# Attention visits of TensorE that carry two pairs, and a product kept in SBUF, in a fused attention and two-layer kernel

## Chip, cores and metric

The kernel runs on one NeuronCore of a Trainium2 chip. The metric is device time in microseconds (us). The engines are named as in the profile: PE is TensorE (matrix products), DVE is VectorE, ACT is ScalarE, POOL is GpSimd, SP is SyncE, which here only issues DMAs.

## What is computed

Three layers follow one another. The first is a linear attention with a decayed state, for 4 batches, 8 heads, 768 steps and a head width of 48:

```
state = alpha[t, :, None] * state + outer(k[t], v[t])      # 48 x 48 per batch and head
y[t]  = q[t] @ state
```

The 8 heads side by side give 3072 tokens of 384 numbers. The second layer is `h = x @ w_in` (384 to 2048), `g = h * cos(h)`, `g @ w_out` (back to 384). The third is `h = max(x @ w1, x @ w2, x @ w3)` (384 to 768), then `h @ w_out`. All data are float32.

## The kernel before, in words

The tokens are cut into six units of 512 (`u` = 0 to 5). A unit of attention is made of four pairs of heads (`p`), so there are 24 pairs; unit 0 has a form of its own (`att0`), and 20 pairs run through `att`. Each has a chunked form of the recurrence. Two scans on DVE (L501, L506) make the decay factors, POOL multiplies them into k and q (L505, L508), PE transposes k (L513) and ACT copies the result to SBUF as `kt` (L516). Then comes a first visit of PE, `akmm`, with 32 products of k and q (L525) and 32 of k and v (L529) in two banks of PSUM. DVE masks the scores into `a` (L534), POOL and DVE bring the state forward (L539 to L551), ACT lays copies of half the state beside it as `z` (L549). A second visit of PE, `values` (L559, L566: 64 small products), makes the outputs in two more banks, and ACT and DVE split them into a high and a low part, in the tile `xt` (L582, L584). Pair 3 of a unit goes through `yy` and is spread over the other three by small DMAs (L591).

The small products use a quarter of the PE array each. The large ones are 128 by 128 by 512 columns. Every factor of the layers is split in a high and a low part, so one product is three of these: high by high, high by low, low by high.

`moe1(i)` is one of the 96 steps of the second layer, 16 for each unit. Nine large products (L604 to L606, three chunks of the inner dimension) fill one PSUM bank with h. ACT makes a whole number from it (L612), DVE reduces the argument (L613), ACT takes the sine (L614), DVE multiplies it with h *into the same bank* (L620), ACT rounds the product to `gh` (L621) and DVE takes the rest as `gl` from the bank (L626). In the steps 0 to 3 the product is kept in the SBUF buffer `q` (L616) and POOL makes the rest. Nine more large products (L631 to L633) add to three accumulators. After the 16th step of a unit the accumulators are emptied through one buffer `yy` to DRAM (L640 to L643). The weights of the second layer come in 32 blocks (L344); ACT, DVE and POOL turn each into a high and a low part (L345 to L354) while the first steps already run. The third layer (`moe2_h`, `moe2_o`, L682 to L710) follows.

PSUM has eight banks. Three are the accumulators; the other five (`NBANK`) are handed out by a planner to h, to the transposes ("t"), to the two visits ("r", "y") and to others, with a limit for each kind (`LIMIT`).

The order of all the work is set before the kernel is built. `Program.op` records every operation with an engine, an estimated duration, what it reads and writes, and a due time in steps. `Program.order` plays these through with a model of the engines, the banks, the DMAs, PE's clock, and the reading of PE's instructions in blocks of 256, takes for each engine the ready operation with the smallest due time, and so fixes one order for each engine. On the chip an engine keeps that order and waits wherever an operand isn't there yet.

Of the kernel before, what the change touches and what calls it, by code (L numbers as in the profile page):

```python
# [26 lines left out]
P = 128  # L27
C = 64
# [24 lines left out]
NQ, NG, NRAW, NRAW1, NTOP, NIN, NKQ, NV, NGS = 3, 2, 3, 4, 2, 3, 2, 3, 3  # L53
# [6 lines left out]
RYS = 9  # L60


GLE1 = 0
# [3 lines left out]
XLE = 3  # L67
MKP = 0
GATE, GSTEP = 1, 2
LOD = (1, 3)  # L70

W1E = 6
MOE_EARLY = 3
EARLY = 1
FIRST = -4
ATT0 = -1
ATTS = 3.3

# [4 lines left out]
class Program:  # L83
# [38 lines left out]
    def order(self, banks, limit):  # L122
# [31 lines left out]
        never = float("inf")  # L154

# [3 lines left out]
        def ready(i):  # L159
            t = ready_at[i]  # L160
            need = opens.get(i, ())
            if need:

                t = max(t, sorted(freed_at[need[0][1]])[len(need) - 1], sorted(bank_free)[len(need) - 1])
            if self.ops[i][6]:
                t = max(t, port_free)
            return t

        for _ in range(n):
# [3 lines left out]
            i = min((self.ops[j][5], j) for j in waiting[e] if ready(j) <= t)[1]  # L173
            waiting[e].remove(i)
            _, dur, nbytes, _, _, _, port, tiled, count = self.ops[i]
            start[i] = t
            if e == "PE":
                if tiled != mode:
                    dur += SWITCH
                    mode = tiled  # L180
                if t - free[e] > IDLE:
                    cold = t + COLD
                dur += min(dur, max(0.0, cold - t) / 2)
                issued += count
                if issued >= block:
                    late = max(0.0, fetched - t - dur * (1.0 - (issued - block) / count))
                    dur += late
                    fetched = t + dur + (FETCH[1] if dma_free > t + dur else FETCH[0])
                    block += BLOCK
# [23 lines left out]
            for u in users[i]:  # L213
# [3 lines left out]
                if not left[u]:  # L217
                    waiting[self.ops[u][0]].append(u)
        self.start, self.end = start, ended
# [15 lines left out]
def mm(n, m):  # L235
    return (n + 0.375 * m) / 2400.0
# [16 lines left out]
def dma(nbytes):  # L253
    return max(nbytes, 15e3)
# [6 lines left out]
HW, LANDED, SLACK = 0.46, 1.6, 5.0  # L261
# [3 lines left out]
def tile_kernel(ctx, tc, aa, qk, vv, wt, outT):  # L265
# [36 lines left out]
    d_b = [ap.tile([PR, 2, N2, D], F32, name=f"d{i}") for i in range(2)]  # L302
    z_b = [ap.tile([PR, N2, D], F32, name=f"z{i}") for i in range(2)]
    kt_b = [ap.tile([P, N2, PR], F32, name=f"kt{i}") for i in range(2)]
# [70 lines left out]
    def att0(k, p, t0):  # L375
        na, nk, nv, n2 = k % NIN, k % NKQ, k % NV, k % 2
        t, kq_, v, kt, s = al_b[na], kq_b[nk], v_b[nv], kt_b[n2], s_b[p]
        vk, kk_ = ("v", nv), nk
        gf, kg = g_b[k % NGS], ("g", k % NGS)
        if k == 2:  # L380
            v, vk = q_b[2][:, 0:2 * N2 * D].rearrange("p (i j e) -> p i j e", i=N2, j=2), ("q", 2)
            kq_, kk_ = q_3.rearrange("p a b -> p (a b)")[0:PR, 0:2 * HB], "q01"
# [10 lines left out]
        tk, sk = ("kt", n2), ("s", p)  # L393
# [87 lines left out]
    def att(u, k, p, t0):  # L481
        m = u * NP + k
        n2, na, nk, nv = m % 2, m % NIN, m % NKQ, m % NV
        t, kq_, v, kt, a, s, d, z, iv = al_b[na], kq_b[nk], v_b[nv], kt_b[n2], a_b[n2], s_b[p], d_b[n2], z_b[n2], inv0[n2]
        vk, kk_ = ("v", nv), nk

        gf, kg = g_b[m % NGS], ("g", m % NGS)
        g = gf.rearrange("p (c t) -> p c t", c=NC)
        fv = t[:, 0:AL].rearrange("p (c t) -> p c t", c=NC)
        kv, qv = kq_[:, 0:HB], kq_[:, HB:]  # L490
        kv3, qv3 = (x.rearrange("p (c t) -> p c t", c=NC) for x in (kv, qv))
        kf, kk, kq = ("inf", na), ("ink", kk_), ("inq", kk_)
        ik, tk, dk = ("iv", n2), ("kt", n2), ("d", n2)
        sk = [("s", p, j) for j in range(2)]
        half = [slice(UP * h, UP * h + D) for h in range(2)]
        first = t0
        op("SP", HW, lambda: nc.sync.dma_start(t, aa[u, p, :, 0:KO]), (), [kf], first - 4.8 + (0.8 if not k else 0), dma(PR * KO * 4), tiled=True)
        op("SP", HW, lambda: nc.sync.dma_start(kq_, qk[u, p]), (), [kk, kq], first - 3.9, dma(PR * 2 * HB * 4), tiled=True)
        op("SP", HW, lambda: nc.sync.dma_start(v, vv[u, p]), (), [vk], first - 3.7, dma(P * HB * 3), tiled=True)
        gate = [("wil", GATE + GSTEP * k)] if u == 1 else []  # L500
        op("DVE", 0.07 + 0.00208 * AL, lambda: ve.tensor_tensor_scan(  # L501
            gf[:, ::-1], t[:, 1:AL + 1][:, ::-1], one0.rearrange("p c t -> p (c t)"), 0.0, ALU.mult, ALU.add), ["one0", kf, *gate], [(*kg, 0), (*kg, 1)], t0 - 1, port=True)
        kgs = [(*kg, 0), (*kg, 1)]
# [4 lines left out]
        op("Pool", pool(HB), lambda: ge.tensor_tensor(qv3, qv3, fv[:, :, 1:], ALU.mult), [kf], [kq], t0 - 1)  # L508
        pk_k, pk = psum("t")
# [5 lines left out]
        op("PE", N2 * 0.08, trans, [kk, "ident"], [pk_k], t0, count=2 * N2)  # L515
        op("Act", act(N2 * PR, True), lambda: se.activation(kt, pk[:, 0:N2 * PR].rearrange("p (a b) -> p a b", a=N2), AF.Copy), [pk_k], [tk], t0)  # L516
        rk, r = psum2("r")
        AO = N2 * D

        def akmm():  # L520
            for i in range(N2):
                for h in range(2):
                    for j in range(2):
                        c, w = 2 * i + h, slice(UP * j, UP * j + D)
                        pe.matmul(r[j][C * h:C * (h + 1), AO + i * C:AO + (i + 1) * C], kv3[w, c], qv3[w, c], start=True, stop=True)  # L525
            for i in range(N2):
                for h in range(2):
                    for j in range(2):
                        pe.matmul(r[h][half[j], i * D:(i + 1) * D], kt[C * h:C * (h + 1), i, UP * j:UP * j + D], v[C * h:C * (h + 1), i, j], start=True, stop=True)  # L529

        op("PE", N2 * (mm4(C) + mm4(D)), akmm, [kk, kq, tk, vk, ("done", n2)], rk, t0 + 0.2, tiled=True, count=128)
        for j in range(2):
            rv = r[j][:, AO:AO + N2 * C].rearrange("p (c t) -> p c t", c=N2)
            op("DVE", dve(HB // 2), lambda j=j, rv=rv: ve.tensor_tensor(a[:, j], rv, tri.to_broadcast([P, N2, C]), ALU.mult),  # L534
               [rk[j], "tri"], [("a", n2, j)], t0 + 0.2)

        kvs = [r[h][0:PR, 0:AO].rearrange("p (b e) -> p b e", b=N2) for h in range(2)]
        gs = [g.rearrange("p (b h) t -> p b h t", h=2)[:, :, h, 0:1].to_broadcast([PR, N2, D]) for h in range(2)]
        op("Pool", pool(N2 * D), lambda: ge.tensor_tensor(d[:, 0], s, gs[0], ALU.mult), [*kgs, *sk], [(dk, 0)], t0 + 0.2)  # L539
        op("DVE", dve(N2 * D), lambda: ve.tensor_tensor(s, kvs[0], d[:, 0], ALU.add), [rk[0], (dk, 0)], sk, t0 + 0.25)  # L540
        op("DVE", dve(N2 * D), lambda: ve.tensor_tensor(d[:, 1], s, gs[1], ALU.mult), [*kgs, *sk], [(dk, 1)], t0 + 0.25, port=True)
        qh = qv.rearrange("p (b h t) -> p b h t", b=N2, h=2)
        for h in range(2):
            w, x = half[h], half[1 - h]
            if u == 1:
                op("Pool", pool(HB // 2), lambda h=h, w=w, x=x: ge.tensor_copy(kv3[w, 0:N2], qh[x, :, h]), [kq], [kk], t0 + 0.25)
            else:
                op("Act", act(HB // 2), lambda h=h, w=w, x=x: se.activation(kv3[w, 0:N2], qh[x, :, h], AF.Copy), [kq], [kk], t0 + 0.25)
            op("Act", act(N2 * D), lambda h=h, w=w, x=x: se.activation(z[w], d[x, h], AF.Copy), [(dk, h)], [("z", n2, h)], t0 + 0.25)  # L549
        if u + 1 < NU:  # L550
            op("DVE", dve(N2 * D), lambda: ve.tensor_tensor(s, kvs[1], d[:, 1], ALU.add), [rk[1], (dk, 1)], sk, t0 + 0.27)  # L551

        yks, y = psum2("r" if u <= RYS else "y")

        def values():
            for i in range(N2):
                for h in range(2):
                    for j in range(2):
                        pe.matmul(y[h][half[j], i * C:(i + 1) * C], v[C * h:C * (h + 1), i, j], a[C * h:C * (h + 1), j, i],  # L559
                                  start=(i == 0), stop=False, skip_group_check=True)  # L560
            for i in range(N2):
                for h in range(2):
                    for j in range(2):
                        w = half[h]
                        dd, qq = (d[w, h, i], qh[w, i, h]) if j == h else (z[w, i], kv3[w, i])
                        pe.matmul(y[h][half[j], i * C:(i + 1) * C], dd, qq, start=False, stop=False, skip_group_check=True)  # L566

        op("PE", N2 * 2 * mm4(C), values,
           [vk, ("a", n2, 0), ("a", n2, 1), *[(dk, h) for h in range(2)], *[("z", n2, h) for h in range(2)], kq, kk], [*yks, ("done", n2)], t0 + 0.3, tiled=True, count=128)
        xa = []  # L570
# [346 lines left out]
```

## Time and profile before

| | |
|---|---|
| median of 3 runs | 780.68 us (780.45 to 780.71) |
| the profiled execution | 780.58 us |
| its span, first to last instruction | 778.7 us |
| PE busy | 768.0 us, 99% of the span, 5863 products |
| DVE, ACT, POOL busy | 55%, 45%, 16% |
| granted clock of PE | 1.00 in every stretch of 20 us but the last (0.96) |

The span is what the trace covers; 1.9 us of the execution lie outside it. PE's busy time is that of overlapping products whose ends are modelled, so how densely PE works is to be read from the distance of starts, not from this share.

### The profile page before, as it was taken

The numbers are of one execution on the slowest core, as the hardware profiler recorded it, in microseconds if no ns is written. First come the engines' busy times: TensorE is split into PE (matmuls) and PEld (weight loads), VectorE is DVE, ScalarE is ACT, GpSimd is POOL, SyncE is SP. The second block draws the span as 40 slices with busy tenths as digits, with TensorE's granted clock in tenths as the row PEclk, the third lists the DMA queues.
The fourth block names the chain that finished last, engine by engine and source line by source line (L and its number), as shares of the span: only waits on it lengthen the run. The fifth ranks groups of instructions, "written<-read, shape, count | busy, mean of one in ns | idle before, by whom it ended". The sixth has DMA issues, their size and how long they took to land.

```text
span 778.7 us, 14199 instructions
## 1 busy us (share of the span) xinstructions
PE 768.0 (99%) x5863; PEld 627.5 (81%) x5863; DVE 425.1 (55%) x718; ACT 348.4 (45%) x671; POOL 127.3 (16%) x133
## 2 busy tenths in 40 slices
PE   8999999999999999999999999999999999999998
PEld 6688887888888888887888888888888888888886
DVE  8889997767675777575567554531221312213121
ACT  5788865546554555555478544421211112111121
POOL 5555432110211111111043200300000000000000
PEclk9999999999999999999999999999999999999999
DMA  9866743212322222121047402320020200200001
GB/s 285 268 191 202 229 122 112 66 54 63 108 65 53 82 89 67 41 90 59 8 142 254 140 0 79 145 81 28 14 95 23 84 27 15 95 13 15 15 26 41
DMA packets 26464, 69.84 MB, mean 90 GB/s; under 512 B 3392, under 2 KB 6464, under 8 KB 26400
## 3 DMA queue, kind: packets, MB, share of 16 engines
q1 hardware_dynamic: 26400, 68.93, 27.7%
q8 instruction: 46, 0.75, 0.4%
q14 instruction: 18, 0.15, 0.1%
HBM read 52.80 MB, written 14.16 MB: 86 GB/s over the span
## 4 chain that ended last, share of the span: by engine, by line
PE 94%; DMA 3%; ACT 1%; DVE 1%; issue 0%; POOL 0%; SPq 0%; ACTq 0%; POOLq 0%; DVEq 0%
PE ps L682 9%; PE ps L683 9%; PE ps L684 9%; PE acc L631 9%; PE ps L604 8%; PE acc L633 8%; PE acc L632 8%; PE ps L605 8%; PE ps L606 8%; PE ps L705 3%; PE ps L707 3%; PE ps L706 3%; PE ps L525 2%; PE ps L559 1%; DMA raw<-in_wt 1%; PE ps L566 1%
## 5 line engine op out<-in xcount | busy, mean ns | idle before, releaser
L631 PE MATMUL acc<-gh,woh 128*128 128x512 f32 x288 | 116.0, 403 | 1.0 <-DVE yy L641 1.0
L604 PE MATMUL ps<-xt,wih 128*128 128x512 f32 x288 | 114.7, 398 | 1.0 <-ACT xt L474 0.8
L605 PE MATMUL ps<-xt,wih 128*128 128x512 f32 x288 | 112.3, 390 | 0.8 <-DVE xt L479 0.8
L632 PE MATMUL acc<-gh,wol 128*128 128x512 f32 x288 | 112.4, 390 | 0.0
L633 PE MATMUL acc<-gl,woh 128*128 128x512 f32 x288 | 112.2, 390 | 0.0
L606 PE MATMUL ps<-xt,wil 128*128 128x512 f32 x288 | 112.1, 389 | 0.0
L613 DVE SCALAR_TENSOR_TENSOR q<-q,ps 128x512 f32<-128x512 int32 x96 | 65.6, 683 | 46.9 <-ACT q L612 46.8
L612 ACT ACTIVATE q<-ps 128x512 int32<-128x512 f32 x96 | 57.2, 596 | 61.6 <-PE ps L606 61.3
L620 DVE TENSOR_TENSOR ps<-q,ps 128x512 f32<-128x512 f32 x92 | 63.7, 692 | 35.8 <-ACT q L614 35.7
L626 DVE TENSOR_TENSOR gl<-ps,gh 128x512 fp32r<-128x512 f32 x92 | 62.9, 687 | 35.6 <-ACT gh L621 35.0
L692 DVE TENSOR_TENSOR ps<-t,ps 128x512 f32<-128x512 f32 x36 | 25.0, 696 | 103.9 <-PE ps L684 103.8
L614 ACT ACTIVATE q<-q 128x512 f32<-128x512 f32 x96 | 60.6, 631 | 39.7 <-DVE q L613 39.4
L621 ACT ACTIVATE gh<-ps 128x512 fp32r<-128x512 f32 x92 | 54.8, 597 | 47.4 <-DVE ps L620 44.0
L693 ACT ACTIVATE h<-ps 128x512 fp32r<-128x512 f32 x36 | 21.6, 600 | 109.7 <-DVE ps L692 109.7
L631 PEld LDWEIGHTS acc<-gh,woh 128*128 128x128 f32 x288 | 54.0, 188 | 13.5 <-DVE yy L641 1.6
L604 PEld LDWEIGHTS ps<-xt,wih 128*128 128x128 f32 x288 | 54.1, 188 | 13.0 <-ACT xt L474 1.2
L633 PEld LDWEIGHTS acc<-gl,woh 128*128 128x128 f32 x288 | 54.1, 188 | 12.0 <-DVE gl L626 0.4
L690 DVE TENSOR_TENSOR t<-t,ps 128x512 f32<-128x512 f32 x36 | 24.8, 688 | 70.9 <-PE ps L684 70.2
L605 PEld LDWEIGHTS ps<-xt,wih 128*128 128x128 f32 x288 | 54.1, 188 | 11.4 <-DVE xt L479 1.1
L606 PEld LDWEIGHTS ps<-xt,wil 128*128 128x128 f32 x288 | 54.1, 188 | 11.4
L632 PEld LDWEIGHTS acc<-gh,wol 128*128 128x128 f32 x288 | 54.1, 188 | 9.9
L710 ACT ACTIVATE y<-ps 128x512 f32<-128x512 f32 x18 | 10.8, 600 | 93.2 <-PE ps L707 93.2
(148 smaller groups left out, 1427.8 us busy)
## 6 DMA issues: line engine op xcount, KB each, us to landing
raw<-in_wt SPq DMA_DIRECT2D x56, 384.0 KB, 3.5
kq<-in_qk SPq DMA_DIRECT2D x22, 448.0 KB, 4.5
x1d<-yy SPq DMA_DIRECT2D x18, 512.0 KB, 2.9
xt<-x1d SPq DMA_DIRECT2D x18, 512.0 KB, 4.2
al<-in_aa SPq DMA_DIRECT2D x23, 228.4 KB, 3.3
outT<-y SPq DMA_DIRECT2D x18, 256.0 KB, 2.0
v<-in_vv SPq DMA_DIRECT2D x23, 192.0 KB, 4.7
xt<-yy SPq DMA_DIRECT2D x30, 64.0 KB, 2.3
```

What stands on the lines that cost most here:

```text
L604: pe.matmul(ps, wi["h"][:, f, cc], xt[:, cc, 0], start=(cc == 0), stop=False)
L605: pe.matmul(ps, wi["h"][:, f, cc], xt[:, cc, 1], start=False, stop=False)
L606: pe.matmul(ps, wi["l"][:, f, cc], xt[:, cc, 0], start=False, stop=(cc == NR - 1))
L613: op("DVE", dve(HB), lambda: ve.scalar_tensor_tensor(q, q.bitcast(I32), -TWOPI, ps, ALU.mult, ALU.add), [hk], [qk], m)
L620: op("DVE", dve(HB), lambda: ve.tensor_tensor(ps, q, ps, ALU.mult), [qk], [hk], m)
L626: op("DVE", dve(HB), lambda: ve.tensor_tensor(gl, ps, gh.bitcast(F32), ALU.subtract), [hk, ("gh", gn)], [("gl", gn)], m)
L631: pe.matmul(acc[c], oh, gh, start=(f == 0), stop=False)
L632: pe.matmul(acc[c], ol, gh, start=False, stop=False)
L633: pe.matmul(acc[c], oh, gl, start=False, stop=(f == NF1 - 1))
L682: pe.matmul(ps, w2t["h"][m][:, f, cc], xt[:, cc, 0], start=(cc == 0), stop=False)
L683: pe.matmul(ps, w2t["h"][m][:, f, cc], xt[:, cc, 1], start=False, stop=False)
L684: pe.matmul(ps, w2t["l"][m][:, f, cc], xt[:, cc, 0], start=False, stop=(cc == NR - 1))
```

## The change

The diff does four things.

- The two visits of a pair are no longer two. From the second pair of unit 2 on, `visit(n, n - 1)` does the first products of pair n and, behind them in the same run of PE, the values of pair n - 1. It takes four of the five banks. The five visits of unit 1's pairs and of the first pair of unit 2 that hold first products alone stay separate, and so do the four values of unit 1 and the very last ones. The transposes and scans of a pair (`turn`) are due one step before its visit.
- From step 16 on (`GLQ`) DVE writes sine times h into the SBUF buffer `q`, and `gh` and `gl` are made from there.
- `d`, `z` and `kt` have one buffer in place of two, and `kq` three in place of two. In unit 0 the transposed k of every other pair lies in a buffer `q`, and one pair no longer borrows two of these.
- The planner's numbers change: a large product costs a little less, a visit has a fixed cost, DMAs of attention get no extra 5 us, a large visit that is overdue keeps others from opening a bank, a visit that would outrun the reading of instructions is put off. The weights of the second layer are due six steps earlier and their loads two steps more; two low parts of unit 0 are made by DVE and not by PE and ACT.

The diff, cut to its core:

```diff
-NQ, NG, NRAW, NRAW1, NTOP, NIN, NKQ, NV, NGS = 3, 2, 3, 4, 2, 3, 2, 3, 3
+NQ, NG, NRAW, NRAW1, NTOP, NIN, NKQ, NV, NGS, ND = 3, 2, 3, 4, 2, 3, 3, 3, 3, 1
-GLE1 = 0
+GLE1, GLQ = 0, 16
-XLE = 3
+XLE = 1
-GATE, GSTEP = 1, 2
+GATE, GSTEP = 1, 1
-W1E = 6
-MOE_EARLY = 3
-EARLY = 1
+W1E = 12
+MOE_EARLY = 4
+EARLY = 3
+VIS, VEND, VQ = 4.0, 13, 0.2
+LARGE, STALL, PATIENT = 2, 0.6, 1.5
+V2, V2S, TA = 16.0, 3.2, 1.0
+NA = (NU - 1) * NP
...
             if need:
-                t = max(t, sorted(freed_at[need[0][1]])[len(need) - 1], sorted(bank_free)[len(need) - 1])
+                for j, due in large.items():
+                    if due + PATIENT < self.ops[i][5] and ready_at[j] <= max(t, free[self.ops[i][0]]):
+                        return never
+                kinds = [k[1] for k in need]
+                t = max(t, sorted(bank_free)[len(need) - 1], *(sorted(freed_at[c])[kinds.count(c) - 1] for c in kinds))
...
-            i = min((self.ops[j][5], j) for j in waiting[e] if ready(j) <= t)[1]
+            def stall(j):
+                n, x = self.ops[j][8], block - issued
+                if n < 128 or x > n:
+                    return 0.0
+                return max(fetched - t - self.ops[j][1] * x / n, FETCH[0] - self.ops[j][1] * (1.0 - x / n) - 0.113 * max(0, BLOCK - n + x))
+
+            i = min((e == "PE" and stall(j) > STALL, self.ops[j][5], j) for j in waiting[e] if ready(j) <= t)[2]
...
 def mm(n, m):
-    return (n + 0.375 * m) / 2400.0
+    return (n + 0.25 * m) / 2400.0
...
-HW, LANDED, SLACK = 0.46, 1.6, 5.0
+HW, LANDED, SLACK = 0.46, 1.6, 0.0
...
+    def visit(an, yn, t0):
+        now, old = (x is not None for x in (an, yn))
...
+        rk, r = psum2("r") if now else ((), ())
+        yks, y2 = psum2("y") if old else ((), ())
...
+            reads += [("ink", nk), ("inq", nk), ("kt",), ("v", nv)]
+            dur, count = dur + 0.87, count + 128
...
+            reads += [("v", nvo), *[("a", yn % 2, j) for j in range(2)], *[(("d", yn % ND), h) for h in range(2)],
+                      *[("z", h) for h in range(2)], ("inq", nko), ("ink", nko)]
+            dur, count = dur + 0.96, count + 128
+
+        def all_parts():
+            if now:
+                akmm()
+            if old:
+                values()
+
+        op("PE", dur, all_parts, reads, sorted({*keys}), t0, tiled=True, count=count)
...
-        if GLE1 <= i < GLP1:
+        if i >= GLQ:
+            op("DVE", dve(HB), lambda: ve.tensor_tensor(q, q, ps, ALU.mult), [hk], [qk], m)
+            op("Act", act(HB), lambda: se.activation(gh, q, AF.Copy), [qk], [("gh", gn)], m)
+            op("DVE", dve(HB), lambda: ve.tensor_tensor(gl, q, gh.bitcast(F32), ALU.subtract), [qk, ("gh", gn)], [("gl", gn)], m, port=True)
+        elif GLE1 <= i < GLP1:
...
+        plan = []
+        for n in range(NP):
+            t = ATT0 + ATTS * n
+            plan += [(t, n, None, t), (t + 0.1, None, n, t + 0.1)]
+        plan += [(t, n, n - 1 if n > NP else None, t - TA) for n, t in ((n, V2 + V2S * (n - NP)) for n in range(NP, 2 * NP))]
+        plan += [(t, n if n < NA else None, n - 1, t - TA) for n, t in ((n, NF1 + VEND + VIS * (n - 2 * NP)) for n in range(2 * NP, NA + 1))]
+        for t, an, yn, tt in plan:
+            if an is not None:
+                at(max(tt - 0.01, FIRST + NP), turn, an, tt)
+            at(max(t, FIRST + NP), visit, an, yn, t)
```

The bodies of `akmm()` and `values()` are those of before, and the operations of DVE, ACT and POOL behind them too; in a visit of two pairs they stand in the order: masks of the new scores, outputs of the old pair, then the state of the new pair.

## Rows read from the trace of the kernel before

**Rows 1.** Page: busy time, share of the span, instructions by engine

```profile
PE 768.0 (99%) x5863; PEld 627.5 (81%) x5863; DVE 425.1 (55%) x718; ACT 348.4 (45%) x671; POOL 127.3 (16%) x133
```

**Rows 2.** Waits of PE: us in total, times, longest one

```profile
PE acc L631 <- DVE yy L641: 1.0, 1, 1.0
PE ps L525 <- ACT kt L516: 1.0, 1, 1.0
PE ps L605 <- DVE xt L479: 0.8, 1, 0.8
PE ps L604 <- ACT xt L474: 0.8, 1, 0.8
```

**Rows 3.** Timeline of PE: first large product, and one undisturbed run (start, duration)

```profile
24.75 0.40 PE L604 MATMUL ps<-xt,wih 128*128 128x512 f32 x1
...
161.09 0.39 PE L604 MATMUL ps<-xt,wih 128*128 128x512 f32 x1
...
163.58 0.39 PE L606 MATMUL ps<-xt,wil 128*128 128x512 f32 x1
```

**Rows 4.** Timeline of PE: a visit of first products between large products

```profile
152.27 0.39 PE L606 MATMUL ps<-xt,wil 128*128 128x512 f32 x1
152.59 0.69 PE L525 MATMUL ps<-kq 48*64 48x64 f32 x32
153.10 0.54 PE L529 MATMUL ps<-v,kt 64*48 64x48 f32 x32
153.57 0.50 PE L631 MATMUL acc<-gh,woh 128*128 128x512 f32 x1
...
154.37 0.40 PE L631 MATMUL acc<-gh,woh 128*128 128x512 f32 x1
```

**Rows 5.** Timeline of PE: the same pair's visit of values

```profile
156.88 0.39 PE L606 MATMUL ps<-xt,wil 128*128 128x512 f32 x1
157.19 0.67 PE L559 MATMUL ps<-a,v 64*48 64x64 f32 x32
...
158.09 0.22 PE L566 MATMUL ps<-kq,d 48*48 48x64 f32 x1
158.24 0.50 PE L604 MATMUL ps<-xt,wih 128*128 128x512 f32 x1
...
159.04 0.40 PE L631 MATMUL acc<-gh,woh 128*128 128x512 f32 x1
```

**Rows 6.** Timeline of ACT: a step of the second layer begins

```profile
163.33 0.60 ACT L612 ACTIVATE q<-ps 128x512 int32<-128x512 f32 x1 [0.67 <-PE ps L606]
```

**Rows 7.** Timeline of DVE: the same step

```profile
163.96 0.69 DVE L613 SCALAR_TENSOR_TENSOR q<-q,ps 128x512 f32<-128x512 int32 x1 [0.58 <-ACT q L612]
165.35 0.70 DVE L620 TENSOR_TENSOR ps<-q,ps 128x512 f32<-128x512 f32 x1 [0.70 <-ACT q L614]
166.71 0.69 DVE L626 TENSOR_TENSOR gl<-ps,gh 128x512 fp32r<-128x512 f32 x1 [0.66 <-ACT gh L621]
```

**Rows 8.** Groups of DVE by line and form: busy us, mean ns, idle before

```profile
L506 DVE TENSOR_TENSOR_SCAN al<-al,inv 112x520 f32<-112x520 f32 x20 | 25.4, 1271 | 0.9
```

**Rows 9.** DMA queues, and issues by line: KB, us from issue to landing

```profile
q8 instruction: 46, 0.75, 0.4%
...
raw<-in_wt SPq DMA_DIRECT2D x56, 384.0 KB, 3.5
...
v<-in_vv SPq DMA_DIRECT2D x23, 192.0 KB, 4.7
```

**Rows 10.** Windows of 20 us: length, PE, PEld, DVE, ACT, POOL busy, clock, DMA

```profile
20.00:40.00 20.00, 18.08 (x175) 13.80 (x174) 16.79 (x29) 15.48 (x33) 11.05 (x13) 1.00 0.80 253
...
80.00:100.00 20.00, 20.00 (x263) 16.33 (x252) 19.65 (x38) 15.59 (x34) 9.72 (x10) 1.00 0.65 194
```

**Rows 11.** Groups of ACT by line and form: the weights' two operations

```profile
L345 ACT ACTIVATE top<-raw 128x384 f16<-128x384 bf16 x56 | 35.7, 643 | 6.6 <-DMA raw<-in_wt 4.8 <-DVE raw L346 1.7
...
L350 ACT ACTIVATE wih<-raw 128x384 fp32r<-128x384 f32 x16 | 8.9, 553 | 0.4 <-DVE raw L346 0.2
```

## What is predicted, before the run

> **What bounds the kernel now.** I read the page first, for who is busy: PE, for 768.0 of the 778.7 us of the span, and no other engine for more than 55% [rows 1]. That share alone doesn't say that PE works densely, so the next view is the timeline of PE, for the distance of starts. In an undisturbed run twelve large products start between 161.09 and 163.58, eleven distances in 2.49 us, so one costs 0.2265 us [rows 3]. There are 18 x 96 = 1728 of them in the second layer and, by the code, 18 x 72 = 1296 in the third: 3024, or 685 us. The first starts at 24.75 [rows 3]. 685 + 24.75 leaves 69 us of the span for all attention behind the start, for waits and for the end. The third view, the waits of PE, shows how little of that is waiting: the four largest behind the start sum to 3.6 us [rows 2]. So attention's small products and what it costs PE to go to them and back are what the change can touch; PE's order is full, and a saving there moves the end by as much, unless a new wait eats it.
>
> **What a visit costs.** From the large product at 152.27 to that at 154.37 there are four large products, counting the first and not the last; 2.10 us less 4 x 0.2265 is 1.19 us for the visit of first products [rows 4]. In the same way the values cost 159.04 - 156.88 - 4 x 0.2265 = 1.25 us [rows 5]. Not all of this is small products. Going in: the first small product starts 0.31 us behind the last large one, where a large one would have started after 0.23, which is 0.08 us [rows 5]; 0.09 in the other visit [rows 4]. Coming out: the 64 small products start from 157.19 to 158.09, 0.014 us apart, but the large one behind the last starts 0.15 us later, so 0.14 is lost; and the three distances behind it take 0.80 in place of 0.68, another 0.12 [rows 5]. The sum is 0.34 us for a way in and out. Inside a visit a change of shape costs nothing that shows: the 32 products of k and q take 0.51 us, the 32 behind them run on in 0.47 with the way out in it [rows 4].
>
> **The merge.** Pairs 0 to 4 of the 20 keep a visit of first products of their own. The other 15 (5 to 19) share one with the values of the pair ahead. So 40 ways in and out become 25, and 15 x 0.34 = 5.1 us of PE's time go. The first four products of a visit are slower too, and how much isn't separated in these rows; I allow up to 0.05 each time, so the bounds are 5.1 and 5.9, and I take 5.4. If the two halves in one run paid for a change of shape between them, the gain would be smaller; nothing in the rows speaks for it. The products, transposes and their sizes stay the same.
>
> **What the merge asks of the banks.** A visit opens four of the five banks at once, where two were opened before. At its start at most one bank may hold h. This is what the second edit is for: in the step shown, ACT begins with the bank at 163.33 [rows 6], the product with the cosine is done at 165.35 + 0.70 = 166.05, and the rest `gl` at 166.71 + 0.69 = 167.40 [rows 7]. The bank is now given back at the first of these, 1.35 us earlier. A step on PE is 18 x 0.2265 = 4.08 us, and h fills for half of it. If h(i), the nine accumulating products of an earlier step, and h(i+1) follow each other, h(i+1) ends 4.08 us behind h(i). Counted from the start of ACT (about 0.2 us behind the end of h), the bank is free after 2.72 us with the new form, 1.2 us ahead of the end of h(i+1), and after 4.07 with the old, just too late. So four banks can be had without a hole. Behind the visit PE has the nine accumulating products of a step ready, 2.04 us, while outputs and masks give banks back. The work itself is the same count of DVE and ACT instructions on other operands; DVE and ACT have room behind step 16, so I cost it at nothing. It would cost where it makes `gl` late: then the accumulating products behind it are late, by the difference.
>
> The Trainium skill has a warning that speaks against the merge: TensorEngine Tiling (Array Packing), Performance Considerations (PSUM Bottleneck), says that tiling makes TensorE faster but not the emptying of PSUM, which may then become the bound. By that the 5.4 us would turn into waits for banks. No wait of PE for a bank of a visit is among the rows of before, where two are opened at a time, so the trace neither has it nor rules it out; the rival below prices it.
>
> **Single buffers.** `kt`, `d`, `z` and one visit: the state work of pair n comes behind visit n and is read by visit n+1, 4 steps (over 16 us) later. Hidden by that distance; were it gone, one would wait for a chain of a few instructions of 0.4 us. The transposes are now due a step ahead of their visit, so the one wait of PE for `kt` in the steady part, 1.0 us [rows 2], should go. The wait of 1.0 us for the emptied accumulator between units stays possible [rows 2]. Against these I set 1.0 us of new small waits, an estimate: the net is 0.
>
> **DMAs.** The same loads are issued. Without the 5 us of slack a load may stand at the head of SP's queue and wait for its buffer, and behind it the small DMAs that fill `xt`; these are needed about three steps, 12 us, behind the values. Attention's end comes some steps later, and so do the loads of the third layer's weights, which have about 15 steps, 60 us, before they are used. Both are costed at nothing.
>
> **The start.** Two low parts of unit 0 leave PE (one large product each, 0.45 us together) and go to DVE. The weights come six steps earlier and rank ahead of unit 0's own evacuations on ACT and DVE. Six steps are 12 blocks, and a block takes ACT 0.64 + 0.55 us [rows 11], 14 us in all, whereas ACT has 4.5 us free and DVE 3.2 between 20 and 40 [rows 10]. In the start PE already waits for the last parts of `xt`, 0.8 and 0.8 us [rows 2], which these weights can push back by a block or three (1.2 us each, so to -3.6 us). On the other side, DVE is at 19.65 of 20 us between 80 and 100 [rows 10], and work taken ahead eases that; waits of 1.6 us and 0.45 us of products could go, +2. I take 0, with these ends.
>
> **Sum.** 780.6 (the profiled execution, 0.1 below the median) - 5.4 = 775.2; I say 775.0. The likeliest case holds 772.5 to 777.5.
>
> **Rivals.**
>
> *Banks become the bound; slower.* If at a visit one h-bank is released late, PE stands still. A scan of DVE, 1.27 us [rows 8], cannot be broken off; if it stands in front of the product with the cosine, it uses up the 1.2 us of room. It decides from 0.36 us a visit on (5.4 / 15), where the kernel is no faster; at half a scan, 0.64 us, the time is 780.6 + 15 x (0.64 - 0.36) = 784.8; at a whole one 794. For it: DVE is the busiest engine behind PE and outputs of the old pair now fall together with masks of the new. Against it: accumulating products can fill 2 us of such a wait, and the planner weighs the banks when it sets the order. 0.17, most of it between 777.5 and 785.
>
> *The start gets worse or better,* as worked out: 778.6 at worst, 773 at best, each somewhat beyond if it falls together with the rest. 0.10 each.
>
> *Reading of instructions.* PE's instructions come by DMA in 46 pieces, 0.75 MB, so 16 KB each, at 0.4% of 16 engines over 778.7 us, or 1.1 us a piece [rows 9]. A product is two instructions (load and multiply), so 256 make a piece, and a merged visit holds 128 products' worth, exactly one piece in about 2.1 us. A DMA from issue to landing takes between that 1.1 us and the 4.7 us of the slowest common load [rows 9]. If a border falls on the edge of a visit, PE could wait up to 4.7 - 2.1 = 2.6 us; bounds 0 and 15 x 2.6 = 39 us. The border has to lie within 2.6 us / 0.113 = 23 instructions of an edge, some 2 in 10 visits, so 3 x 1.3 = 4 us if the order did nothing about it, and the time 779. 0.05.
>
> The Trainium skill, Runtime: NRT & Kernel Launch (Instruction fetch mechanics), has instructions refilled in blocks of 256 and the cost of a border mostly hidden; the count and size of the pieces agree, and no row here shows a fetch that PE waited for. By it this rival would be worth nothing.
>
> *The merge does not save:* if the loss at the way out belongs to each group of small products and not to the change of mode, the time is 780.6. Rows 4 speak against it, where one group follows another without a hole. Within the 0.58 of the forecast I keep nothing for it, and count it with the first rival.
>
> **Chances.** Forecast 0.58; banks 0.17 (faster 0.04, same 0.04, slower 0.09); start better 0.10; start worse 0.10 (0.04, 0.02, 0.04); reading 0.05 (0.02, 0.01, 0.02). Faster by over 0.2% (1.6 us, about what a measurement of this kernel can tell from no change) 0.78, within it 0.07, slower 0.15. From 771 to 781 about 2 in 10 are left out: banks above it and a few ends.
>
> **What would show it.** In the trace after: 15 runs of 128 small products, each costing about 2.10 us against large ones, not 2.44; PE behind step 16 without waits at visits; the product with the cosine written to `q` 80 times; first large product at 24.75 within 2 us. Wrong would make it: waits of PE for DVE or ACT at the first large product behind or the first small one in a visit, over 0.3 us each; a hole in the middle of a visit beside a piece of instructions; the first large product beyond 27.

## The result

The changed kernel takes 774.23 us (773.59 to 774.97, four runs) against 780.57 for the kernel before on the same chip: a ratio of 0.9917, interval 0.9905 to 0.9929. Measured once more on another chip (e8 below), it gave 0.9916. Forecast were 775.0 and 771 to 781.

The first lines of the page after, busy time by engine, answer to [rows 1]:

```profile
span 772.1 us, 14185 instructions
PE 762.5 (99%) x5863; PEld 626.0 (81%) x5863; DVE 429.4 (56%) x720; ACT 348.4 (45%) x669; POOL 125.3 (16%) x133
```

PE does the same 5863 products, in a span that is 6.6 us shorter. As before, its busy share of 99% says nothing of where they went; the distance of starts does. The timeline of PE after, at a visit of two pairs (start, duration), answers to [rows 4, 5]:

```profile
152.74 0.39 PE L691 MATMUL acc<-gl,woh 128*128 128x512 f32 x1
153.06 0.69 PE L556 MATMUL ps<-kq 48*64 48x64 f32 x32
153.58 0.54 PE L560 MATMUL ps<-v,kt 64*48 64x48 f32 x32
153.94 0.63 PE L574 MATMUL ps<-a,v 64*48 64x64 f32 x32
...
154.80 0.22 PE L581 MATMUL ps<-kq,d 48*48 48x64 f32 x1
154.94 0.50 PE L658 MATMUL ps<-xt,wih 128*128 128x512 f32 x1
...
155.75 0.39 PE L658 MATMUL ps<-xt,wih 128*128 128x512 f32 x1
```

The values (L574) follow the products of k and v (L560) after 0.36 us, where the large product came after 0.47 in [rows 4]: no way out in between. Four large products start from 152.74 on and ahead of 155.75; 3.01 - 4 x 0.2265 = 2.10 us for the whole visit. The two of before cost 1.19 + 1.25 = 2.44 [rows 4, 5]. Counted over six large products behind each visit, where the last trace of the slow start has gone, they are 2.47 and 2.10. All 15 visits of two pairs cost 2.10, so the merge is worth 15 x 0.34 to 0.37 = 5.1 to 5.6 us of the 6.6; 5.6 is the full count.

Waits of PE after, us in total, times, longest, those of the first large products on, answer to [rows 2]; behind 115 us there is none:

```profile
PE ps L556 <- POOL kq L520: 0.8, 1, 0.8
PE ps L658 <- ACT woh L365: 0.6, 1, 0.6
PE acc L691 <- DVE gl L684: 0.4, 1, 0.4
PE ps L659 <- DVE xt L494: 0.2, 1, 0.2
```

The two waits of 1.0 us in [rows 2], for `kt` and for the emptied accumulator, are gone. They cost more than their 1.0 us each. The timeline of PE before, at the one for the accumulator (start, duration, in brackets the idle time ahead and what ended it):

```profile
122.65 0.39 PE L606 MATMUL ps<-xt,wil 128*128 128x512 f32 x1
122.88 0.55 PE L513 MATMUL ps<-ident,kq 112*128 112x112 f32 x4
124.41 0.50 PE L631 MATMUL acc<-gh,woh 128*128 128x512 f32 x1 [0.98 <-DVE yy L641]
```

From 122.65 to 124.41 are 1.76 us; around four transposes that stand alone and have no such wait behind them it is 0.55 everywhere behind 115 us, so 1.21 are lost for a bracket of 0.98.

So the loss is counted here by starts: what the distances between starts of large products exceed 0.2265 us by, less the price of every visit and of every four transposes (0.41). Behind 115 us it is 3.5 us before and 0.7 after, 2.9 us less. Ahead of 115 us it is 3.9 before and 6.0 after, 2.2 us more (work of unit 0 that is the same in both is in these two numbers). The first large product starts at 24.37, 0.4 earlier than in [rows 3]; that can't be put down to the change, since in e8, the same kernel, it starts at 24.99, 0.2 later. The sum is 5.6 + 2.9 - 2.2 + 0.4 = 6.7. The timeline of PE after shows two places of the loss ahead of 115 us, two idle-fillers that the planner put there (L909) and a hole at 85 us:

```profile
32.71 1.02 PE L909 MATMUL ps<-ident 128*128 128x512 f32 x2
...
85.01 0.39 PE L660 MATMUL ps<-xt,wil 128*128 128x512 f32 x1
85.47 0.50 PE L689 MATMUL acc<-gh,woh 128*128 128x512 f32 x1
85.80 0.40 PE L690 MATMUL acc<-gh,wol 128*128 128x512 f32 x1
86.63 0.50 PE L691 MATMUL acc<-gl,woh 128*128 128x512 f32 x1 [0.43 <-DVE gl L684]
86.96 0.40 PE L689 MATMUL acc<-gh,woh 128*128 128x512 f32 x1
```

From 85.01 to 86.96 there are four large products in 1.95 us, 1.0 us more than they need, for a bracket of 0.43. The starts of products count, not the idle time: a product is shown for 0.39 to 0.40 us though the next one can start after 0.23, so the first 0.17 us of a hole don't show as idle, and behind each of the two holes here (85.47 and 86.63) the next start comes after 0.33.

How the bank fares in a step after, DVE's timeline, answers to [rows 7]:

```profile
214.45 0.69 DVE L667 SCALAR_TENSOR_TENSOR q<-q,ps 128x512 f32<-128x512 int32 x1 [0.61 <-ACT q L666]
215.83 0.69 DVE L670 TENSOR_TENSOR q<-q,ps 128x512 f32<-128x512 f32 x1 [0.70 <-ACT q L668]
```

ACT's L666 of this step starts at 213.82, so the bank is free at 215.83 + 0.69 = 216.52, after 2.70 us; 2.72 were forecast.

### The profile page after: what moved, and what is told of

The parts are those of the page before. It is cut to its first block, busy times and chain, and to the rows that moved or that the text cites. A ratio compares the mean times of both kernels' runs of the same rounds, so it can differ in the third digit from the quotient of the medians.

```text
span 772.1 us, 14185 instructions
## 1 busy us (share of the span) xinstructions
PE 762.5 (99%) x5863; PEld 626.0 (81%) x5863; DVE 429.4 (56%) x720; ACT 348.4 (45%) x669; POOL 125.3 (16%) x133
## 4 chain that ended last, share of the span: by engine, by line
PE 88%; DVE 1%; ACT 1%; issue 0%; DVEq 0%; ACTq 0%
PE ps L740 10%; PE ps L742 10%; PE ps L741 9%; PE acc L689 8%; PE acc L691 8%; PE ps L658 8%; PE acc L690 8%; PE ps L659 7%; PE ps L660 7%; PE ps L765 3%; PE ps L763 3%; PE ps L764 3%; PE ps L556 1%; PE ps L574 1%; PE ps L581 1%; PE ps L530 1%
## 5 line engine op out<-in xcount | busy, mean ns | idle before, releaser
L689 PE MATMUL acc<-gh,woh 128*128 128x512 f32 x288 | 114.0, 396 | 0.1
L691 PE MATMUL acc<-gl,woh 128*128 128x512 f32 x288 | 112.4, 390 | 0.4 <-DVE gl L684 0.4
L666 ACT ACTIVATE q<-ps 128x512 int32<-128x512 f32 x96 | 57.1, 595 | 59.6 <-PE ps L660 58.0
L672 DVE TENSOR_TENSOR gl<-q,gh 128x512 fp32r<-128x512 f32 x80 | 57.8, 724 | 32.9 <-ACT gh L671 30.5
L670 DVE TENSOR_TENSOR q<-q,ps 128x512 f32<-128x512 f32 x80 | 54.7, 684 | 27.5 <-ACT q L668 26.5
L671 ACT ACTIVATE gh<-q 128x512 fp32r<-128x512 f32 x80 | 50.2, 629 | 35.1 <-DVE q L670 32.1
L691 PEld LDWEIGHTS acc<-gl,woh 128*128 128x128 f32 x288 | 54.1, 188 | 12.7 <-DVE gl L684 1.3
```

The lines of the kernel that those rows point to most:

```text
L672: op("DVE", dve(HB), lambda: ve.tensor_tensor(gl, q, gh.bitcast(F32), ALU.subtract), [qk, ("gh", gn)], [("gl", gn)], m, port=True)
L689: pe.matmul(acc[c], oh, gh, start=(f == 0), stop=False)
L691: pe.matmul(acc[c], oh, gl, start=False, stop=(f == NF1 - 1))
```

## The experiments

e1 to e4, e5 to e8 and e9 to e12 ran on one chip each. Ratios are to the kernel before on that chip; a difference to the changed kernel in us is the difference of the ratios times 780.6.

**e1_split: two visits for each pair again, all else as changed.**

```diff
+        for n in range(NP, NA):
+            t = V2 + V2S * (n - NP) if n < 2 * NP else NF1 + VEND + VIS * (n - 2 * NP)
+            plan += [(t, n, None, t - TA), (t + 0.1, None, n, t + 0.1)]
```

in place of the two lines of `plan` with visits of two pairs.

> Every pair has its two visits of PE again; all else is the changed kernel (banks, GLQ, planner, start). If the way in and out of the small products is what was saved, 15 of them come back at 0.37 us (2.47 for two visits against 2.10 for one in the two traces): 5.6 us, so about 779.8, and the trace shows visits of 1.21 and 1.27 us and none of 2.10. If the gain came from the order and from fewer waits instead, the time stays within 1 us of 774.2.

Measured: 1.0009 (0.9996 to 1.0022), 781.65 us. The whole gain is gone, and 1.6 us beyond the 5.6 with it. In its trace every visit of first products behind 115 us but two costs 1.21 and every visit of values but one 1.27 us, none 2.10, and PE waits nowhere behind 115 us. So the price of the ways in and out came back as forecast, and the waits of before did not. The 1.6 beyond lie in the first 115 us, where the order came out another way as well (loss by starts 9.4 us in the profiled execution, which took 783.85, against 6.0); this run doesn't separate them.

**e3_mid_large: a large product in the middle of each visit of two pairs.**

```diff
             if now:
                 akmm()
+            if now and old:
+                pe.matmul(y2[1].rearrange("p (a b) -> p a b", b=P), wi["h"][:, 0, 0], wi["h"][:, 0:4, 0], start=True, stop=True)
             if old:
                 values()
```

> The order of the changed kernel; in each of the 15 visits of two pairs one extra large product (128 by 128 by 512, of weights already in SBUF, into a bank that the values then overwrite) stands between the first products and the values. If each change between large and small products has its price, a visit costs 0.23 for the product and 0.37 for another way in and out: 15 x 0.60 = 9.0 us, about 783.2, visits of 2.70. If the loss belonged to each group of small products, only 15 x 0.23 = 3.4 us, 777.6.

Measured: 1.0035 (1.0023 to 1.0048), 784.12 us. Against the changed kernel's 0.9917 that is 1.18%, 9.2 us; 9.0 were expected from the price of the way, 3.4 from the rival. The timeline of PE of this run:

```profile
155.53 0.39 PE L693 MATMUL acc<-gl,woh 128*128 128x512 f32 x1
155.84 0.69 PE L556 MATMUL ps<-kq 48*64 48x64 f32 x32
156.36 0.54 PE L560 MATMUL ps<-v,kt 64*48 64x48 f32 x32
156.83 0.50 PE L591 MATMUL ps<-wih 128*128 128x512 f32 x1
157.26 0.66 PE L574 MATMUL ps<-a,v 64*48 64x64 f32 x32
```

With one large product between, L574 starts 0.90 us behind L560 in place of 0.36. The visit costs 2.68 us in all, 0.58 more than 2.10; 0.23 of that is the product, 0.35 the second way. PE's order is the same, product for product, so this is the cleanest measurement of the price.

**e2_no_glq: the product with the cosine in the PSUM bank again.**

```diff
-GLE1, GLQ = 0, 16
+GLE1, GLQ = 0, 96
```

> The product with the cosine is written to the PSUM bank again in every step from 4 on (GLQ = 96); the merge stays. If the bank has to be given back earlier for four banks to be free at a visit, PE now waits at visits or their due times slip: at 0.1 to 0.5 us for each of 15 visits 1.5 to 7 us more, 776 to 781. If the 2 us of accumulating products cover it, the time stays within 1 us of 774.2.

Measured: 1.0122 (1.0098 to 1.0146), 791.26 us: 16 us slower than the changed kernel, far more than expected of it. Its waits of PE behind 115 us, and one of them in the timeline:

```profile
PE acc L689 <- DVE yy L699: 4.6, 4, 2.0
PE ps L574 <- DVE gl L684: 2.2, 2, 1.1
PE ps L556 <- DVE gl L684: 2.2, 1, 2.2
PE ps L658 <- DVE gl L684: 1.3, 4, 0.6
```

```profile
199.09 0.39 PE L660 MATMUL ps<-xt,wil 128*128 128x512 f32 x1
201.64 0.69 PE L556 MATMUL ps<-kq 48*64 48x64 f32 x32 [2.16 <-DVE gl L684]
```

A visit (L556) stands for 2.16 us until DVE has made `gl` (L684) *from the bank*: it waits for the bank, since it reads nothing that `gl` makes. These waits sum to 10 us, 5.7 of them for `gl`; the other 4.6 are for emptied accumulators. By starts, 13.0 us more than in the changed kernel are lost behind 115 us. The planner made another order for this kernel, too, so not each of them is the bank's.

**e5_glq_only: this one edit in the kernel before.** The branch for steps from 16 on, as in the diff of the change, and nothing else.

> The kernel before with only one edit: from step 16 the product with the cosine stays in SBUF and DVE makes the rest from there; two visits for each pair, planner and start as before. In the trace of the changed kernel PE waits some 2.8 us less behind 105 us than before. If that comes from the bank given back earlier, this kernel is faster by 1 to 3 us, 777.5 to 779.5 against 780.6. If the bank matters only where four are opened at once, it stays within 0.7 us.

Measured: 0.9976 (0.9966 to 0.9986), 778.98 us: 1.9 us faster. Of the two waits of 1.0 us in the steady part [rows 2] one of 0.5 is left:

```profile
PE acc L635 <- DVE yy L645: 0.5, 1, 0.5
```

So the edit helps where two banks are opened at once, too. Why is open: neither of the two waits was for a bank, and the planner changed the order of PE with the edit.

**e11_no_reserve: the planner no longer keeps banks for an overdue visit.**

```diff
-LARGE, STALL, PATIENT = 2, 0.6, 1.5
+LARGE, STALL, PATIENT = 9, 0.6, 1.5
```

> The changed kernel without the planner's rule that an overdue visit of two pairs keeps other work from opening a bank (LARGE = 9, so no visit counts as large). If four free banks don't come by themselves, visits are put off while h takes bank after bank, late outputs make PE wait between units: 1 to 6 us, 775 to 780. If they come by themselves, since the bank of h is given back within a step, it stays within 0.7 us.

Measured: 1.0126 (1.0108 to 1.0143), 791.73 us: 16 us slower than the changed kernel. Windows of this run (length; PE, PEld, DVE, ACT, POOL busy; clock, share of the DMA engines, GB/s), and then the same windows of the changed kernel:

```profile
105.00:180.00 75.00, 74.19 (x509) 60.93 (x507) 47.51 (x78) 37.25 (x67) 4.10 (x4) 1.00 0.11 36
180.00:205.00 25.00, 15.74 (x530) 13.60 (x530) 20.97 (x39) 10.98 (x28) 12.46 (x12) 0.73 0.77 223
205.00:405.00 200.00, 199.49 (x2088) 165.00 (x2089) 133.35 (x229) 108.81 (x209) 28.62 (x29) 1.00 0.19 58
```

```profile
105.00:180.00 75.00, 75.00 (x816) 62.05 (x815) 60.38 (x105) 41.68 (x82) 16.58 (x15) 1.00 0.28 82
180.00:205.00 25.00, 25.00 (x353) 20.73 (x352) 19.89 (x36) 16.42 (x33) 3.38 (x4) 1.00 0.31 104
205.00:405.00 200.00, 200.00 (x2030) 165.12 (x2029) 129.69 (x220) 108.35 (x208) 30.92 (x30) 1.00 0.21 61
```

Between 105 and 180 us PE does 509 products, not 816: the visits of unit 2, due there, don't come; only the rule on banks was taken from the order. They come from 174 us on, when the next large products need their outputs (205.51 below). PE has little else to do by then, and the chain of a visit (scans, POOL, transposes, copy) lies open again and again:

```profile
183.54 0.60 PE L530 MATMUL ps<-ident,kq 112*128 112x112 f32 x4 [1.36 <-POOL kq L517]
...
192.20 1.13 PE L556 MATMUL ps<-kq 48*64 48x64 f32 x32 [1.93 <-DVE s L636]
...
205.51 0.47 PE L658 MATMUL ps<-xt,wih 128*128 128x512 f32 x1 [1.64 <-DMA xt<-yy]
```

PE is busy for 15.74 of these 25 us, and the granted clock is 0.73 on the mean. Behind 205 us the run is as dense as the changed kernel's.

**e6_no_stall_rule: no visit is put off for the reading of instructions.** `STALL` is 99.

> The changed kernel without the planner's rule that puts off a visit which would outrun the reading of instructions (its limit of 0.6 us set to 99). If borders of pieces at an edge of a visit cost PE time, a few visits show a hole of 0.5 to 2.5 us, 1 to 4 us together: 775 to 778 against 774.2. If reading is hidden anyway, visits stay at 2.10 and the time within 0.7 us, but for what another order does to the start.

Measured: 0.9913 (0.99 to 0.9925), 774.11 us, no difference. The 15 visits cost 2.10 to 2.11 and come in the same places, so the rule had nothing to put off here: the order of PE, DVE, ACT and POOL is that of the changed kernel, and the run is one more repeat of it. No hole stands in a visit of either kernel; what a border in a worse place would cost, no run shows.

**e4_old_start: the five numbers of the start as before** (W1E 6, MOE_EARLY 3, EARLY 1, GSTEP 2, XLE 3).

> The five numbers of the start are those of before (W1E 6, EARLY 1, MOE_EARLY 3, GSTEP 2, XLE 3); merge, GLQ and planner stay. By the two traces PE loses some 1.7 us more in the first 115 us of the changed kernel than before, beside the merge. If the earlier weights are the cause, this one is faster by up to 1.7 us, about 772.5. If they are not, it stays or is slower, 774 to 777.

Measured: 0.9925 (0.9912 to 0.9938), 776.04 us. The interval overlaps that of the changed kernel; the old numbers don't give the lost time back, and the loss by starts ahead of 115 us is 6.0 us as in the changed kernel. What the trace shows beside the start is one wait of 1.3 us at the first visit of two pairs, for DVE's product (L670).

**e10_old_numbers: two of the planner's estimates as before.**

```diff
-    return (n + 0.25 * m) / 2400.0
+    return (n + 0.375 * m) / 2400.0
-HW, LANDED, SLACK = 0.46, 1.6, 0.0
+HW, LANDED, SLACK = 0.46, 1.6, 5.0
```

> The changed kernel with two of the planner's old numbers: a large product costs (512 + 0.375 x 128) / 2400 again and loads of attention get 5 us of slack. The order alone changes. If the better order of the changed kernel comes from these numbers, PE waits more: 1 to 4 us, 775 to 778. If the merge and the banks carry the gain, it stays within 1 us.

Measured: 0.9958 (0.9944 to 0.9972), 777.79 us: 0.41%, 3.2 us, slower than the changed kernel, with intervals apart. PE waits nowhere behind 115 us here either; the waits that it has lie ahead of that, the largest behind the first large product this one:

```profile
PE acc L691 <- POOL gl L676: 0.9, 2, 0.7
```

By starts, about half of its additional loss lies there (7.8 us against 6.0) and half behind 115 us (2.5 against 0.7), in small delays that the view of waits doesn't list. So these numbers are worth 3 us by the order alone, with the same instructions.

**e7, e9, e12: attempts at a faster kernel.** Most of the time lost ahead of 115 us lies between 60 and 100 us (1.4 of the 2.2), where DVE is busy for 19.5 and 18.7 of 20 us. e7 merges three visits of unit 1 as well (`plan += [(t, n, n - 1 if n else None, t - TA)]`, GLQ = 4), e9 lets POOL make the rest `gl` up to step 9 (GLP1 = 10), e12 moves half of DVE's low parts of weights to POOL (LOD = (3,)).

> The changed kernel with three more visits of two pairs: in unit 1 too the first products of a pair share a visit with the values of the pair ahead (the last values of the unit stay alone), and the product with the cosine stays in SBUF from step 4. By the price of a way in and out it is faster by 3 x 0.37 = 1.1 us, 773.1. If DVE, which has next to no idle time there, and the banks decide in the first 110 us, it is slower by 1 to 4 us, 775 to 778.

> The changed kernel with the rest gl of the steps 4 to 9 made by POOL from SBUF, as it is in the steps 0 to 3 (GLP1 = 10), and not by DVE from the bank: 6 x 0.69 us less for DVE between 50 and 90 us, where DVE is busy for 18.6 to 19.5 of 20 us and PE waits 1.1 us in all for gl at 85 us. If DVE is what PE waits for there, this is faster by 0.5 to 1.5 us: 773. If POOL, with 9 to 12 of 20 us busy and 1.3 us for each, comes later than DVE did, it stays or is slower: 774 to 777.

> The changed kernel with half of DVE's weight blocks moved: of four blocks, one and not two has its low part made by DVE from PSUM; the other goes to POOL (LOD = (3,)). That is 8 x 0.55 us less for DVE and 8 x 1.0 us more for POOL in the first 90 us. If DVE sets the early waits it is faster by 0.5 to 1.5 us, 773; if POOL's part of the loads' ring of four buffers is what sets the weights, slower by 0.5 to 3, 775 to 777.

Measured: e7 0.9978 (0.9968 to 0.9987), 779.15 us; e9 0.9910 (0.9897 to 0.9924), 774.69; e12 0.9995 (0.9977 to 1.0014), 780.92. e7 is 4.8 us slower than the changed kernel, and its timeline shows the first merged visit of unit 1 waiting for a bank:

```profile
62.22 0.69 PE L556 MATMUL ps<-kq 48*64 48x64 f32 x32 [2.31 <-DVE q L670]
```

e9 removes the hole at 85 us (its waits have no L691 any more), but another comes at 108 us, and the time is that of the changed kernel. e12 takes load from DVE (16.7 and 15.9 of 20 us busy from 60 to 100, 19.5 and 18.7 in the changed kernel), and is slower all the same, with more waits for `gl`: so less load on DVE doesn't by itself make the start faster. What sets its pace, these runs don't settle.

**e8_same_again: the changed kernel without an edit,** on the chip of e5 to e7.

> The changed kernel once more, without an edit, on this chip: it gives the size that the other comparisons of this call are read against. 0.9917 of the kernel before, about 774.2; visits of 2.10; all theories expect the same.

Measured: 0.9916 (0.9903 to 0.9929), 774.19 us, visits of 2.10.

No version beats the changed kernel by more than the intervals.

## Why the prediction was right, point by point

- *What a visit costs.* Right. 0.34 us for a way in and out, taken from single distances of starts, became visits of 2.10 us, the number that was named. e3 buys the same way again and pays for it.
- *The merge.* Right in mechanism and size: 5.4 taken, 5.1 to 5.6 measured in the visits. The rival that it doesn't save is refuted by e3.
- *What it asks of the banks.* The sum was right, that a bank comes back 2.7 us behind ACT's start and four can be had without a hole. The step "so I cost it at nothing" was right for the kernel as it stands, but the text took too lightly what the cover is. It takes both the earlier return of the bank (e2: 16 us) and an order that keeps h from taking banks (e11: 16 us); lacking either, the kernel is slower than before by 1.2 to 1.3%. The rival was priced at 784.8 with half a scan a visit and 794 with a whole one; 791 and 792 came, but not by scans: in e2 by the bank that is held for `gl`, in e11 by visits that were put off as a whole. The Trainium skill, TensorEngine Tiling (Array Packing), Performance Considerations (PSUM Bottleneck), has it that tiling doesn't speed up the emptying of PSUM, which may become the bottleneck. The changed kernel has no wait for a bank behind 115 us; the 5.7 us of e2 come from how long one bank is held for `gl`, not from the rate of emptying, so no run here tests that rule.
- *The edit by itself.* Mis-sized: the second edit was seen only as a help for the merge. Alone it is worth 1.9 us (e5), in which waits that were there before get fewer; by what way isn't shown.
- *Waits.* The net of 0 was the wrong size: 2.0 us of waits behind 115 us went, 2.9 us by starts, and 0 came there, not 1.0. That the wait for `kt` would go was right; that for the accumulator went too.
- *The start.* The net of 0 was off by 1.8 us, inside the ends of -3.6 and +2: the first large product came 0.4 earlier, by chance as e8 shows, and 2.2 us were lost between it and 115 us. The named cause, the earlier weights, is not borne out: with the old numbers (e4) the same is lost. What the cause is stays open. The planner's estimates, which the prediction passed over, matter more (e10: 3.2 us).
- *Reading of instructions.* As forecast, not seen: no hole beside or in a visit. The Trainium skill, Runtime: NRT & Kernel Launch (Instruction fetch mechanics), calls the cost of a border mostly hidden; no hole beside any of the 15 visits speaks against it, and no run here puts a border in a worse place.
- The forecast was 0.8 us too high, 1.1 against the profiled execution (773.87). That the merge came out at 5.6 for 5.4 is its mechanism; that the rest nearly fits is partly luck: 2.9 us were gained behind 115 us and 1.8 lost ahead of it, where both had been set to 0.

## What to carry to other kernels

Where an engine does the same instructions and is never idle, look at the distance of starts around a change between kinds of work: what PE lost at each change was 0.34 to 0.37 us, forty times over, and no view of waits named it. Putting two visits in one saves that, but doubles what has to be free at its start; price that resource first, find the edit that gives it back earlier, and see that the order keeps it for the visit. And one long hole can come from work that was put off, not from work that got slower: compare how many instructions each stretch does, as in e11, ahead of looking at single waits.

## What the hardware showed that was not expected

- A visit that PE doesn't wait in costs the same each time to 0.01 us: behind 115 us 1.21, 1.27 and 2.10 us in the kernels before and after. With the one large product between, a way in and out costs 0.35 us in e3 in place of 0.37.
- DVE's subtraction `gl` has one operand in PSUM before (L626) and both in SBUF after (L672). While POOL does nothing, it takes 0.69 us either way (686 and 688 ns on the mean). Beside an instruction of POOL it still takes 690 ns with one operand in PSUM, at most 694 (27 times), but 813 ns on the mean with both in SBUF (23 of 80 times): seven take 0.82 to 1.38 us, six of them beside POOL's L520 and one beside its L369. The mean over all 80 and the longest one, with the POOL instruction beside it:

```profile
L672 DVE TENSOR_TENSOR gl<-q,gh 128x512 fp32r<-128x512 f32 x80 | 57.8, 724 | 32.9 <-ACT gh L671 30.5 <-PE acc L690 2.0
```

```profile
140.74 1.38 DVE L672 TENSOR_TENSOR gl<-q,gh 128x512 fp32r<-128x512 f32 x1
139.44 2.12 POOL L520 TENSOR_TENSOR kq<-kq,al 112x512 f32<-112x512 f32 x1
```

PE waits for none of these here. The second edit thus trades a bank that comes back earlier for a `gl` that is sometimes longer beside POOL.

- ACT's `gh` took 597 ns from PSUM and 629 ns from SBUF.
- In e11 the granted clock was 0.73 on the mean in the 25 us in which PE was busy for 15.74, so partly at the lower of its two levels, 1.2 GHz; it is 1.00 in the other windows of e11 and of the changed kernel shown above.
